# Two attention blocks on one core: the order in which an operation's several semaphore waits are stated

## The chip, the cores and the metric

The kernel runs on one core of a Trainium2 chip. The metric is the time of one execution on the device in microseconds (us); the number given for a kernel is the median of several runs. The engines are named as in the profile: PE is TensorE, PEld its weight loads, DVE is VectorE, ACT is ScalarE, POOL is GpSimd, SP is SyncE, which here only issues transfers.

## The reference

Two independent blocks are computed, and their outputs are put side by side along the last axis.

```python
def _A_ref(x, wqkv, wo):                      # x: 1 x 2048 x 1024, 32 heads of 32
    qkv = (x @ wqkv).reshape(B, S, 3, H, Dh).transpose(2, 0, 3, 1, 4)
    q, k, v = qkv[0], qkv[1], qkv[2]
    p = softmax(einsum('bhqd,bhkd->bhqk', q, k) * Dh ** -0.5)
    o = einsum('bhqk,bhkd->bhqd', p, v)
    return o.transpose(0, 2, 1, 3).reshape(B, S, D) @ wo

def _B_ref(x, wq, wk, wv, wo, beta):          # 4 segments of 512 rows, causal inside each
    for s in range(4):
        p = softmax(einsum('bhqd,bhkd->bhqk', qs, ks) * scale + mask)
        a_dot = einsum('bhqk,bhkd->bhqd', p, vs)
        num, den = phi(qs) @ M, phi(qs) @ z + 1e-6      # memory of the segments before
        o = g * num / den + (1 - g) * a_dot             # g = sigmoid(beta), per head
        M, z = M + phi(ks)^T @ vs, z + sum(phi(ks))
    return o @ wo                                       # phi(t) = t + 1 if t > 0 else exp(t)
```

## The kernel before

Everything is computed in pieces of a few tenths of a microsecond to one microsecond. Attention runs in sets of four tiles of 128 keys by 512 columns: PE writes the scores into PSUM (L1190; eight matmuls of 256 columns, their operands in KQ_A or KQ_B), ACT takes the exponential of 1024 columns at a time into P (L1288), and PE multiplies P with V (L1401) and with ones (L1408) for the sums. For block A one tile in some sets goes another way: DVE copies the scaled scores into Y (L1236), POOL squares them into Z (L1245) and turns Z into Pc (L1246), which stands for the exponential. Between the sets PE does the projections, each as runs of matmuls of 512 columns (L829 and, with other shapes, L1764 and L1866) that DVE copies out of PSUM (L1608, L1876), and the output products. Six PSUM banks in three slots serve the scores, two banks the projections and sums; a bank is written again when its reader has read it, so that PE waits for ACT or DVE, and these for PE. Weights (W_A, W_B, Wv_B, Wo_B) come by DMA on SP's queue, into one or two buffers.

What each engine does, and in which order, is settled when the program is built. `Prog.op` records every operation with the operations it depends on; `schedule` sets the order on each engine from planned durations, `rearrange` shifts it by a table, and `retime` gives each operation its planned start and end. `programs` then makes each engine's list of waits and operations. An operation needs what its dependencies on other engines (and, where needed, its own) have done. The dependencies are sorted by the time at which the plan has them met; going through them from the last to the first, a semaphore is noted in `need` only if nothing noted or waited for before already tells that it is met. So `need` begins with the wait that is planned to be met last. Its entries become `("w", semaphore, value)` items ahead of the operation, and `emit` turns each into a `wait_ge` in that order (`run_split` for ACT, whose list can branch).

About 390 operations of PE, 156 of DVE and 120 of POOL have more than one wait; ACT has 9 on the way that is run (it has a second list of the same work for data that the first does not suit), SP none.

## Time and profile before

| | us |
|---|---|
| median of 3 runs | 1057.81 |
| lowest, highest | 1056.15, 1058.79 |
| span of the profiled execution | 1056.3 |
| PE busy | 1023.3 (97%) |
| ACT busy | 1001.5 (95%) |
| POOL busy | 724.7 (69%) |
| DVE busy | 703.4 (67%) |

The span goes from the first to the last instruction of the profiled execution; the time of that execution is not listed apart from the runs. The granted TensorE clock is full over the whole span. The ends of matmuls are modelled, so that a busy PE is not one at its peak. Instructions that only wait are not among the profile's rows: what they cost shows in the distance between the end of what was waited for and the start of what waited. Times in the timeline are from the start of the span, and a row gives start, duration, engine, line, operation, output and input, count, and in brackets the idle time before it with what ended it ("issue" where the profile finds no releaser).

### The profile page before, as it was taken

Reading aid. Unit: us, or ns where it says so; the run is one execution under the profiler, and the core shown is the slowest. Engines: PE = TensorE matmul, PEld = TensorE weight load, DVE = VectorE, ACT = ScalarE, POOL = GpSimd, SP = SyncE. Lnnn points to the kernel's source line nnn. Section 1 sums busy time; section 2 is a strip of 40 time slices with the busy share of each in tenths; the row PEclk is TensorE's granted clock in tenths of the full one; section 3 lists DMA queues with packets and bytes.
Section 4 is the critical chain, followed back from the end, with each engine's and each line's share of the span. In section 5 each row is a group of like instructions: output and inputs, shape, how many; then the busy total and the mean of one; then the engine's idle time right before and its main releaser. Section 6 shows DMA issues by size and latency. Waiting matters only on the chain.

```text
span 1056.3 us, 54941 instructions
## 1 busy us (share of the span) xinstructions
PE 1023.3 (97%) x25091; PEld 551.2 (52%) x25092; DVE 703.4 (67%) x1451; ACT 1001.5 (95%) x1193; POOL 724.7 (69%) x999
## 2 busy tenths in 40 slices
PE   9999999999999999999999999999999999999998
PEld 4456455566555454556555445556555445445544
DVE  3457577666656878696755879777646887674444
ACT  5999999999999999898999999999999999999995
POOL 1005567666766888888956899888755878985551
PEclk9999999999999999999999999999999999999999
DMA  9213351007112530033241221133041433122002
GB/s 175 47 43 93 68 138 28 16 13 160 49 41 70 123 85 17 3 62 92 67 113 44 78 65 38 27 75 91 27 113 35 125 102 113 33 68 73 28 29 66
DMA packets 172377, 72.24 MB, mean 68 GB/s; under 512 B 135536, under 2 KB 170352, under 8 KB 172144
## 3 DMA queue, kind: packets, MB, share of 16 engines
q1 hardware_dynamic: 169776, 67.93, 26.3%
q8 instruction: 197, 3.23, 1.3%
q10 hardware_dynamic: 2368, 0.79, 0.3%
q14 instruction: 36, 0.29, 0.1%
HBM read 45.36 MB, written 11.80 MB: 54 GB/s over the span
## 4 chain that ended last, share of the span: by engine, by line
PE 56%; ACT 32%; DVE 4%; POOL 3%; SPq 3%; issue 1%; DMA 0%; ACTq 0%; POOLq 0%; DVEq 0%
ACT P L1288 32%; PE ps L829 27%; PE ps L1190 11%; PE ps L1401 8%; PE ps L1408 8%; SPq L1572 2%; POOL Z L1245 2%; DVE Y L1236 1%; PE ps L1866 1%; PE ps L1638 1%; POOL Pc L1246 1%; DVE T L1515 1%; DMA W_A<-in_A_wqkv_dram 0%; DVE PKQ_B L1925 0%; POOL P L1317 0%
## 5 line engine op out<-in xcount | busy, mean ns | idle before, releaser
L1288 ACT ACTIVATE P<-ps 128x1024 bf16<-128x1024 f32 (+1 forms) x1178 | 991.5, 999 | 33.6 <-PE ps L1190 18.7
L1245 POOL TENSOR_TENSOR Z<-Y 128x512 f32<-128x512 f32 x287 | 304.2, 1062 | 202.2 <-DVE Y L1236 177.7
L1408 PE MATMUL ps<-P,onesb 128*32 128x256 bf16 (+1 forms) x4386 | 300.8, 270 | 0.7 <-issue 0.6
L1401 PE MATMUL ps<-P,V_A 128*32 128x256 bf16 x3618 | 257.7, 274 | 0.7 <-issue 0.3
L1236 DVE TENSOR_SCALAR Y<-ps 128x512 f32<-128x512 f32 x239 | 163.7, 685 | 110.1 <-PE ps L1190 90.5
L1190 PE MATMUL ps<-KQ_A 32*128 32x256 bf16 x4096 | 204.1, 272 | 12.4 <-ACT P L1288 5.5
L1246 POOL TENSOR_SCALAR Pc<-Z 128x512 bf16<-128x512 f32 x239 | 155.6, 654 | 11.0 <-PE ps L1190 0.2
L1190 PEld LDWEIGHTS ps<-KQ_A 32*128 32x128 bf16 x4096 | 62.8, 92 | 163.9 <-ACT P L1288 108.7
L1408 PEld LDWEIGHTS ps<-P,onesb 128*32 128x32 bf16 x4386 | 128.8, 96 | 30.1 <-issue 14.8
L829 PE MATMUL ps<-xT_B,W_B 128*32 128x512 bf16 (+1 forms) x2132 | 138.7, 372 | 0.8 <-DVE OT_B L1948 0.2
L829 PE MATMUL ps<-xT_A,W_A 128*32 128x512 bf16 (+1 forms) x2020 | 131.4, 370 | 2.2 <-DMA W_A<-in_A_wqkv_dram 1.1
L1401 PEld LDWEIGHTS ps<-P,V_A 128*32 128x32 bf16 x3618 | 108.1, 96 | 34.3 <-issue 14.3
L1401 PE MATMUL ps<-Pc,V_A 128*32 128x256 bf16 x478 | 123.1, 273 | 0.4 <-ACT P L1288 0.2
L1408 PE MATMUL ps<-Pc,onesb 128*32 128x256 bf16 x478 | 122.8, 273 | 0.0
L1317 POOL TENSOR_SCALAR_AFFINE_SELECT P<-P 128x768 bf16<-128x768 bf16 (+1 forms) x96 | 76.3, 803 | 34.7 <-ACT P L1288 33.1
L1515 DVE STREAM_TRANSPOSE T<-ps 128x512 f32<-128x512 f32 x122 | 86.3, 708 | 14.0 <-PE ps L1408 11.9
L829 PEld LDWEIGHTS ps<-xT_B,W_B 128*32 128x32 bf16 x2132 | 50.3, 96 | 45.5 <-issue 19.6
L829 PE MATMUL ps<-Wo_B,OT_B 128*32 128x512 bf16 (+1 forms) x1080 | 71.6, 370 | 0.2 <-DVE rc L1518 0.2
L829 PE MATMUL ps<-Wv_B,xT_B 128*32 128x512 bf16 (+1 forms) x1096 | 70.3, 367 | 0.2
L829 PEld LDWEIGHTS ps<-xT_A,W_A 128*32 128x32 bf16 x2020 | 47.4, 96 | 42.1 <-issue 12.5
L1533 POOL TENSOR_TENSOR T<-T,rc 128x256 bf16<-128x256 f32 x74 | 48.9, 663 | 29.6 <-DVE rc L1518 25.8
L1608 DVE CAST KQ_A<-ps 128x512 bf16<-128x512 f32 x60 | 41.3, 689 | 40.5 <-PE ps L829 40.1
(109 smaller groups left out, 1201.0 us busy)
## 6 DMA issues: line engine op xcount, KB each, us to landing
Wv_B<-in_B_wv_dram SPq DMA_DIRECT2D x32, 256.0 KB, 3.5
W_B<-in_B_wk_dram SPq DMA_DIRECT2D x32, 256.0 KB, 3.3
W_B<-in_B_wq_dram SPq DMA_DIRECT2D x32, 256.0 KB, 4.1
Wo_B<-in_B_wo_dram SPq DMA_DIRECT2D x32, 256.0 KB, 3.5
out_dram<-outsb SPq DMA_DIRECT2D x56, 128.0 KB, 1.9
W_A<-in_A_wqkv_dram SPq DMA_DIRECT2D x14, 256.0 KB, 3.6
ot_a_scratch<-OTst SPq DMA_DIRECT2D x52, 64.0 KB, 2.3
xT_A<-ot_a_scratch SPq DMA_DIRECT2D x6, 512.0 KB, 4.8
```

Of the source, the lines that this page charges most:

```text
L829: ins = e.matmul(out[r], w[:, r], x, start=start, stop=stop, tile_position=(0, 32 * t), skip_group_check=True)
L1190: ins = e.matmul(out, kap, qap, start=st, stop=True, tile_position=(32 * h, 0), skip_group_check=True)
L1236: o = self.dve(lambda e: e.tensor_scalar(Y[:, :], src, SCALE, MID, ALU.mult, ALU.add), 512, key - 9.0, [self.bank[bank]], [rY], fixed=0.15)
L1245: self.pool(lambda e: e.tensor_tensor(Z[:, :], Y[:, :], Y[:, :], ALU.mult), 512, key, [rY], [rZ], rate=0.58)
L1246: return self.pool(lambda e: e.tensor_scalar(dst, Z[:, :], C2, REST, ALU.mult, ALU.add), 512, key, [rZ], [rP], rate=TS_RATE)
L1288: a = self.act(guarded if early and not free else lambda e: e.activation(dst, src, ACT.Exp, scale=SCALE), cols, key, rd, wr, fixed=EXP_FIXED)
L1317: self.pool(lambda e: e.affine_select(v, v, pattern=pat, compare_op=ALU.is_ge, fill=0.0, base=0, channel_multiplier=-1), 2 * nd * P, key + ...
L1401: ins = e.matmul(self.ps[32 * h:32 * h + 32, 512 * obk + q0:512 * obk + q0 + nq], v, p, start=first, stop=last, tile_position=(0, 32 * h), ...
L1408: ins = e.matmul(self.ps[32 * h:32 * h + 32, lcol + q0:lcol + q0 + nq], self.onesb[:, 0:32], p, start=False, stop=last, tile_position=(0, ...
L1515: self.dve(lambda e: e.transpose(T2[:, :], src), 512, k - NORM_K, [obk.res], [ro, rl], fixed=0.17)
L1533: self.pool(lambda e: e.tensor_tensor(half.rearrange("p (b r) -> p b r", r=32), ov, bc, ALU.mult), QC, k, [ro, rr], [rl], rate=0.435)
L1608: self.dve(lambda e: e.tensor_copy(dst, src), 512, key, [self.at(b)], rdst, fixed=0.155)
```

## The change

The waits noted in `need` are stated in the order in which they were noted, the one planned to be met last first. Before, they were stated from the other end. Which semaphores and values are waited for, the operations, their order and their buffers stay as they were.

```diff
                     for x in reversed(deps):
                         s, v = target(x)
                         if k.get(id(s), 0) < v:
                             need.append((s, v))
...
-                    for s, v in reversed(need):
+                    for s, v in need:
                         prog[e].append(("w", s, v))
```

On PE, about 98 us into the span, a set of scores (L1190) and a projection of block B (L829) stand close together, both with two waits. s_ACT, s_DVE and s_POOL are the semaphores that count what these engines have done; d_WB01 is that of the DMA which brings the second piece of W_B. Before:

```order
L1190 MATMUL ps<-KQ_A 128x256 [waits s_ACT,s_DVE]
L1190 MATMUL ps<-KQ_A 128x256 x7
L1401 MATMUL ps<-Pc,V_A 32x256
L1401 MATMUL ps<-P,V_A 32x256 x3
L1408 MATMUL ps<-Pc,onesb 32x256
L1408 MATMUL ps<-P,onesb 32x256 x3
L829 MATMUL ps<-xT_B,W_B 32x512 [waits s_DVE,d_WB01]
L829 MATMUL ps<-xT_B,W_B 32x512 x3
L1401 MATMUL ps<-P,V_A 32x256 x4
```

And after:

```order
L1190 MATMUL ps<-KQ_A 128x256 [waits s_DVE,s_ACT]
L1190 MATMUL ps<-KQ_A 128x256 x7
L1401 MATMUL ps<-Pc,V_A 32x256
L1401 MATMUL ps<-P,V_A 32x256 x3
L1408 MATMUL ps<-Pc,onesb 32x256
L1408 MATMUL ps<-P,onesb 32x256 x3
L829 MATMUL ps<-xT_B,W_B 32x512 [waits d_WB01,s_DVE]
L829 MATMUL ps<-xT_B,W_B 32x512 x3
L1401 MATMUL ps<-P,V_A 32x256 x4
```

For the scores, ACT's semaphore stood ahead and DVE's on the first matmul's weight load; now DVE's stands ahead and ACT's is the load's own. For the projection, DVE's stood ahead and the DMA's was the load's own; now the DMA's stands ahead.

On POOL, about 876 to 882 us into the span, squares (Z) and their second step (Pc) stand in turn. A square waits for DVE, which makes Y, and for POOL itself, which must have read the Z that is written again. Before:

```order
L1245 TENSOR_TENSOR Z<-Y 128x512 [waits s_DVE,s_POOL]
L1246 TENSOR_SCALAR Pc<-Z 128x512 [waits s_POOL]
L1245 TENSOR_TENSOR Z<-Y 128x512 [waits s_POOL,s_DVE]
L1246 TENSOR_SCALAR Pc<-Z 128x512
L1245 TENSOR_TENSOR Z<-Y 128x512 [waits s_DVE,s_POOL]
L1246 TENSOR_SCALAR Pc<-Z 128x512 [waits s_POOL]
L1520 TENSOR_SCALAR rc<-rc,gc 128x8
L1245 TENSOR_TENSOR Z<-Y 128x512 [waits s_POOL,s_DVE]
```

And after:

```order
L1245 TENSOR_TENSOR Z<-Y 128x512 [waits s_POOL,s_DVE]
L1246 TENSOR_SCALAR Pc<-Z 128x512 [waits s_POOL]
L1245 TENSOR_TENSOR Z<-Y 128x512 [waits s_DVE,s_POOL]
L1246 TENSOR_SCALAR Pc<-Z 128x512
L1245 TENSOR_TENSOR Z<-Y 128x512 [waits s_POOL,s_DVE]
L1246 TENSOR_SCALAR Pc<-Z 128x512 [waits s_POOL]
L1520 TENSOR_SCALAR rc<-rc,gc 128x8
L1245 TENSOR_TENSOR Z<-Y 128x512 [waits s_DVE,s_POOL]
```

In each pair the two names have changed places; which of the two was ahead before differs from square to square, as the plan has one or the other met last. Operations with a single wait are as they were.

## The prediction

> **What bounds the kernel now.** I read the page first, then the list of waits, the chain of waits in order of time, and last the timeline in windows of a fifth of a microsecond, where two neighbouring rows show how long an engine takes to start once it is released.

> ```profile
> span 1056.3 us, 54941 instructions
> PE 1023.3 (97%) x25091; PEld 551.2 (52%) x25092; DVE 703.4 (67%) x1451; ACT 1001.5 (95%) x1193; POOL 724.7 (69%) x999
> PE 56%; ACT 32%; DVE 4%; POOL 3%; SPq 3%; issue 1%; DMA 0%; ACTq 0%; POOLq 0%; DVEq 0%
> ```

> Two engines are nearly full, ACT with exponentials and PE with everything that feeds and follows them, and the chain that ended last changes between the two, with short pieces of DVE and POOL between. No engine alone is the bound. Such a program pays for every hand-over on that chain: an operation ends, its semaphore rises, and the next engine starts a little later.

> ```profile
> ACT P L1288 <- PE ps L1190: 18.7, 37, 1.2
> ACT P L1288 <- PE ps L1408: 11.6, 18, 1.6
> PEld ps L1190 <- ACT P L1288: 130.9, 368, 1.1
> PEld ps L829 <- issue: 62.2, 289, 0.5
> ```

> ACT stood for PE only 55 times (37 + 18), for 30.3 us together; PE's weight loads stood for ACT 368 times, and those of L829 289 times for 62.2 us where the profile names no releaser ("issue"). What the change touches is the last tenth of a microsecond of such waits.

> ```profile
> 45.42 8.36 ACT P L1288 x9
> ...
> 920.69 113.88 ACT P L1288 x139
> ```

> These are the first and the last of 17 pieces of over 4 us in which the chain runs through exponentials back to back, 336 us together. There no hand-over counts; it counts in the 720 us that are left.

> **What the change moves.** It moves no operation, adds none and takes none away. An operation with several waits keeps the same ones, in the opposite order. The rows on the change above show how the built program holds them: one wait sits on the operation itself, the others stand ahead of it as wait instructions. Before, the semaphore planned to be met last stands ahead, alone, and the early one sits on the operation; after the change it is the other way round. So the question is what it costs when the late semaphore is met by the instruction of its own, and not by the operation.

> PE first. A weight load with one wait, after the DVE operation that releases it:

> ```profile
> 40.78 0.69 DVE L1608 CAST KQ_A<-ps 128x512 bf16<-128x512 f32 x1 [2.02 <-PE ps L829]
> 41.53 0.12 PEld L829 LDWEIGHTS ps<-xT_A,W_A 128*32 128x32 bf16 x8 [0.20 <-DVE KQ_A L1608]
> 1047.56 0.69 DVE L2109 TENSOR_TENSOR KQ_B<-ps,KQ_B 128x512 bf16<-128x512 f32 x1 [0.53 <-PE ps L829]
> 1048.30 0.10 PEld L829 LDWEIGHTS ps<-W_A,xT_A 128*32 128x32 bf16 x4 [0.21 <-DVE KQ_B L2109]
> ```

> DVE ends at 41.47 and 1048.25; the load starts 0.06 and 0.05 later. Now loads with two waits, where DVE's semaphore is the late one and stands ahead:

> ```profile
> 77.72 0.69 DVE L1608 CAST KQ_A<-ps 128x512 bf16<-128x512 f32 x1 [0.67 <-PE ps L829]
> 78.53 0.13 PEld L1866 LDWEIGHTS ps<-Wv_A,xT_A 128*128 128x128 bf16 x2 [0.27 <-issue]
> 97.67 0.69 DVE L1608 CAST KQ_B<-ps 128x512 bf16<-128x512 f32 x1
> 98.47 0.13 PEld L829 LDWEIGHTS ps<-xT_B,W_B 128*32 128x32 bf16 x4 [0.15 <-issue]
> 983.57 0.68 DVE L1236 TENSOR_SCALAR Y<-ps 128x512 f32<-128x512 f32 x1
> 984.36 0.15 PEld L1190 LDWEIGHTS ps<-KQ_A 32*128 32x128 bf16 x8 [0.38 <-ACT P L1288]
> ```

> DVE ends at 78.41, 98.36 and 984.25, the loads start 0.12, 0.11 and 0.11 later: **0.06 us more** for each. The load at 98.47 is the one shown with its waits in the section on the change.

> DVE shows the difference inside one kind of operation, Y at L1236, each with a wait for PE and one for POOL:

> ```profile
> 877.65 1.04 POOL L1245 TENSOR_TENSOR Z<-Y 128x512 f32<-128x512 f32 x1
> 878.73 0.69 DVE L1236 TENSOR_SCALAR Y<-ps 128x512 f32<-128x512 f32 x1 [0.95 <-POOL Z L1245]
> 918.26 1.04 POOL L1245 TENSOR_TENSOR Z<-Y 128x512 f32<-128x512 f32 x1
> 919.41 0.69 DVE L1236 TENSOR_SCALAR Y<-ps 128x512 f32<-128x512 f32 x1 [2.46 <-POOL Z L1245]
> ```

> POOL ends at 878.69 and 919.30, and Y starts 0.04 and 0.11 later. In the first the plan had PE's semaphore last, so POOL's sits on the operation; in the second POOL's stands ahead. The difference is **0.07 us**. POOL the same, Z with one wait and then with two:

> ```profile
> 911.87 0.69 DVE L1236 TENSOR_SCALAR Y<-ps 128x512 f32<-128x512 f32 x1 [0.44 <-PE ps L1190]
> 912.64 1.04 POOL L1245 TENSOR_TENSOR Z<-Y 128x512 f32<-128x512 f32 x1 [0.19 <-DVE Y L1236]
> 117.24 0.68 DVE L1236 TENSOR_SCALAR Y<-ps 128x512 f32<-128x512 f32 x1
> 118.07 1.04 POOL L1245 TENSOR_TENSOR Z<-Y 128x512 f32<-128x512 f32 x1 [2.02 <-DVE Y L1236]
> 878.73 0.69 DVE L1236 TENSOR_SCALAR Y<-ps 128x512 f32<-128x512 f32 x1 [0.95 <-POOL Z L1245]
> 879.57 1.08 POOL L1245 TENSOR_TENSOR Z<-Y 128x512 f32<-128x512 f32 x1 [0.29 <-DVE Y L1236]
> ```

> Y ends at 912.56, 117.92 and 879.42; Z starts 0.08, 0.15 and 0.15 later, again **0.07 us**.

> [...]

> **The sum.** I followed the chain back from ACT's last instruction through the trace, at each step to what came last: a release with the delays above, or the instruction before on the same engine. On it lie 145 starts with several waits that were released by the wait standing ahead: 97 on PE (first 78.53; 984.36 is the last that DVE releases), 28 on DVE (919.41 among them), 20 on POOL (first 118.07, last 879.57). At the full price that is 97 x 0.06 + 28 x 0.07 + 20 x 0.07 = 5.8 + 2.0 + 1.4 = 9.2 us. Two things come off. Of the 145, 35 (26 on PE, 9 on DVE) lie inside the 17 long pieces above, where the profile's own chain has ACT running through; I count those at nothing, the exponential before being what is late next. That leaves 71 x 0.06 + 19 x 0.07 + 20 x 0.07 = 4.3 + 1.3 + 1.4 = 7.0 us. And on 11 places of the chain (6 on PE, 3 on DVE, 2 on POOL; 878.73 is one) the early-planned semaphore came last in fact: there the change puts the late one ahead, which costs 6 x 0.06 + 5 x 0.07 = 0.7 us. **7.0 - 0.7 = 6.3 us saved.**

> Costed at nothing: ACT, whose few operations with several waits are not on the chain; SP, whose waits keep their order; and the wait that now stands ahead, which by plan was met earlier, so that it is passed while the engine still works at what is before it. Where that cover is missing, the price is the 0.06 to 0.07 us just counted. Nothing new is queued behind a waiting instruction: the same engine waits for the same pair, and behind it stands what stood there.

> The span, 1056.3, is 1.5 us under the median of the runs shown, 1057.81, and the fastest run took 1056.15, so the profiled execution was an ordinary one and the saving may be taken off the median: 1057.8 - 6.3 = **1051.5 us**. Differences under 0.3%, 3.2 us, cannot be told from none here.

> **The rivals.**

> *The gain is taken up by the other chains (0.12).* PE and ACT are both nearly full, so beside the chain run others that are almost as long. For it speaks that ACT stands for PE only 55 times. If the end moves only where ACT stood, and every second of these has one dear start ahead of it, the gain is 55 x 0.06 / 2 = 1.6 us: 1056.2, which would read as no change. Against it speaks that the 110 places are spread over the whole span and that each shortens PE's chain and ACT's alike.

> *The plan's order is wrong more often than now (0.10).* When some engines start earlier, semaphores that lay 0.1 us apart may change places, and an operation whose early-planned one now comes last gains nothing. If a third of the 110 flip, 110 / 3 x 0.063 = 2.3 us are lost: 4.0 saved, 1053.8.

> *The late semaphore standing ahead is the cheap way, and the change makes it dear (0.05).* As the source reads, the wait stated last is next to the operation, and the change moves the late one away from it. If the last stated wait sat on the operation in what the chip executes, the 145 places would each become dearer by 0.06 to 0.07: 9.2 us, less the 0.7 of the 11 places that would then gain, 1066.3. It decides if the dear starts above have another reason than the place of the wait, such as a longer decode of this kind of load; L1236, where the same operation starts after 0.04 and after 0.11, speaks against that. [...]

> *It does nothing (0.03).* If the waits are sorted again on the way to the chip, both programs are one: 1057.8.

> **How the numbers follow.** My forecast has 0.70, and 1051.5 is its value. The range reaches from the full price of all 145 places, 1057.8 - 9.2 = 1048.6, to the absorbed gain, 1056.2; that leaves out the last two rivals, 0.08, and the tails. Faster by over 0.3% (under 1054.6): the forecast and the flipped order, 0.80. Within 0.3%: absorbed or nothing, 0.15. Slower: 0.05.

> **What would show it.** In the changed profile the load of the second W_B piece (98.47 before) should start 0.05 after its CAST, Y at L1236 behind POOL 0.04 and Z behind Y 0.08 in nearly every case with two waits; the gain should grow evenly up to about 900 us, and little in the last 130. ACT's 30.3 us of standing for PE should fall by some microseconds, and the 62.2 us of L829's loads put down to "issue" too. The working is wrong if these starts are as short as I say and the span still stays within 3 us (then the hand-overs were not on what sets the end), and the reading of the order is wrong if the starts at 0.11 have grown in number.

## The result, and the profile after

The changed kernel took 1051.33 us (median of 6 runs, 1050.78 to 1052.71), the kernel before, beside it, 1058.17 us (6 runs, 1056.15 to 1060.88). The ratio is 0.9937, its 95% interval 0.9924 to 0.9949: by this ratio 6.7 us faster, 5.4 to 8.0. The same kernel, run again as the last of the experiments, gave 0.9934 (0.9920 to 0.9947).

The page of the changed kernel first, its span, the engines, and the chain by engine:

```profile
span 1049.4 us, 54941 instructions
PE 1019.2 (97%) x25091; PEld 548.0 (52%) x25092; DVE 703.0 (67%) x1451; ACT 999.0 (95%) x1193; POOL 725.7 (69%) x999
PE 62%; ACT 29%; DVE 3%; SPq 2%; POOL 1%; issue 1%; DMA 1%; ACTq 0%; DVEq 0%; POOLq 0%
```

The same work, as full as before, in a span that is 6.9 us shorter. DVE and POOL have a smaller part of the chain than before (4% together, from 7%), ACT too (29%, from 32%), and PE a larger one (62%, from 56%). The list of waits, with us in total, times, and the longest:

```profile
PEld ps L1190 <- ACT P L1288: 118.7, 343, 1.2
PEld ps L829 <- issue: 50.3, 235, 1.5
...
ACT P L1288 <- PE ps L1190: 16.1, 31, 1.2
...
ACT P L1288 <- PE ps L1408: 10.0, 17, 1.6
```

ACT stands for PE 26.1 us in place of 30.3 (28.6 in a second profile of the changed kernel). The weight loads of L829 for which the profile named no releaser are 54 fewer and stand 11.9 us less. I read these as loads whose late semaphore was met by a wait instruction ahead of them, which is not among the profile's rows; the first two loads shown next, of L1866 and L829, are of this kind.

Now the starts themselves, at the places of the prediction. PE's loads with two waits, in the timeline of the changed kernel:

```profile
77.84 0.69 DVE L1608 CAST KQ_A<-ps 128x512 bf16<-128x512 f32 x1 [0.76 <-PE ps L829]
78.59 0.11 PEld L1866 LDWEIGHTS ps<-Wv_A,xT_A 128*128 128x128 bf16 x2 [0.21 <-DVE KQ_A L1608]
...
97.52 0.69 DVE L1608 CAST KQ_B<-ps 128x512 bf16<-128x512 f32 x1
98.26 0.10 PEld L829 LDWEIGHTS ps<-xT_B,W_B 128*32 128x32 bf16 x4
...
976.56 0.68 DVE L1236 TENSOR_SCALAR Y<-ps 128x512 f32<-128x512 f32 x1
977.39 0.15 PEld L1190 LDWEIGHTS ps<-KQ_A 32*128 32x128 bf16 x8 [0.35 <-DVE Y L1236]
```

DVE ends at 78.53 and 98.21, and the loads start 0.06 and 0.05 later, where it was 0.12 and 0.11; for the first the profile now names DVE as the releaser where it had said "issue". The third, 977.39, starts 0.15 after DVE's end at 977.24, where it was 0.11. After the loads of L829 ahead of it (at 976.94, and at 983.88 before) it starts 0.45 later, where it was 0.48: so the work ahead seems to hold it now, and of the 0.06 only 0.03 is gained here. Of the three loads that the prediction shows, two have the full price. DVE's Y behind POOL, and POOL's Z behind Y:

```profile
911.57 1.04 POOL L1245 TENSOR_TENSOR Z<-Y 128x512 f32<-128x512 f32 x1
912.65 0.69 DVE L1236 TENSOR_SCALAR Y<-ps 128x512 f32<-128x512 f32 x1 [2.38 <-POOL Z L1245]
...
871.25 1.09 POOL L1245 TENSOR_TENSOR Z<-Y 128x512 f32<-128x512 f32 x1
872.44 0.69 DVE L1236 TENSOR_SCALAR Y<-ps 128x512 f32<-128x512 f32 x1 [1.00 <-POOL Z L1245]
873.21 1.14 POOL L1245 TENSOR_TENSOR Z<-Y 128x512 f32<-128x512 f32 x1 [0.29 <-DVE Y L1236]
```

Y at 912.65 (919.41 before) starts 0.04 after POOL, not 0.11. Y at 872.44 (878.73 before) is the one whose early-planned semaphore comes last: it starts 0.10 after POOL, where it was 0.04. The two have changed places, to a hundredth. Z starts 0.08 after Y's end at 873.13, where it was 0.15. The same holds over the whole trace, counted from the rise of the semaphore. Of POOL's starts on a release by DVE, 46 of 152 came 0.12 to 0.14 us after it, and now 2 of 149. Of DVE's starts on a release by POOL, 7 of 34 came 95 or 96 ns after it, and now 1 of 36, the Y at 872.44; nearly all others came after 23 to 25 ns.

Last, where in the span the time went. Pieces of the chain that are the same stretch of work in both kernels, first before, then after:

```profile
221.26 16.68 ACT P L1288 x19
...
449.40 23.33 ACT P L1288 x27
...
666.68 23.24 ACT P L1288 x27
...
808.00 24.56 ACT P L1288 x29
...
1045.35 6.29 PE ps L829 x116
```

```profile
219.85 16.68 ACT P L1288 x19
...
447.14 23.16 ACT P L1288 x27
...
661.99 23.16 ACT P L1288 x27
...
802.43 24.57 ACT P L1288 x29
...
913.84 27.80 ACT P L1288 x33
...
1038.52 6.29 PE ps L829 x116
```

The stretches begin 1.4, 2.3, 4.7, 5.6 and 6.8 us earlier. The run of exponentials that began at 920.69 begins at 913.84, 6.85 earlier, and 125 us later the lead is still 6.83. The gain is made in small steps all along, and none in the last eighth.

### The profile page after: what moved, and what is told of

The parts are those of the page before. It is cut to its first block, busy times and chain, and to the rows that moved or that the text cites. A ratio compares the mean times of both kernels' runs of the same rounds, so it can differ in the third digit from the quotient of the medians.

```text
span 1049.4 us, 54941 instructions
## 1 busy us (share of the span) xinstructions
PE 1019.2 (97%) x25091; PEld 548.0 (52%) x25092; DVE 703.0 (67%) x1451; ACT 999.0 (95%) x1193; POOL 725.7 (69%) x999
## 4 chain that ended last, share of the span: by engine, by line
PE 62%; ACT 29%; DVE 3%; SPq 2%; POOL 1%; issue 1%; DMA 1%; ACTq 0%; DVEq 0%; POOLq 0%
PE ps L829 30%; ACT P L1288 29%; PE ps L1190 12%; PE ps L1401 9%; PE ps L1408 9%; SPq L1572 2%; PE ps L1866 1%; DVE Y L1236 1%; PE ps L1638 1%; DVE T L1515 1%; DMA W_A<-in_A_wqkv_dram 1%; POOL Z L1245 0%; POOL P L1317 0%; DVE KQ_B L1608 0%; DVE sqB L1621 0%
## 5 line engine op out<-in xcount | busy, mean ns | idle before, releaser
L1288 ACT ACTIVATE P<-ps 128x1024 bf16<-128x1024 f32 (+1 forms) x1178 | 989.0, 1020 | 29.4 <-PE ps L1190 16.1
L1245 POOL TENSOR_TENSOR Z<-Y 128x512 f32<-128x512 f32 x287 | 305.4, 1067 | 195.3 <-DVE Y L1236 182.3
L1408 PE MATMUL ps<-P,onesb 128*32 128x256 bf16 (+1 forms) x4386 | 300.1, 270 | 0.0
L1236 DVE TENSOR_SCALAR Y<-ps 128x512 f32<-128x512 f32 x239 | 163.8, 685 | 108.7 <-PE ps L1190 90.0
L1190 PE MATMUL ps<-KQ_A 32*128 32x256 bf16 x4096 | 204.1, 273 | 12.1 <-ACT P L1288 6.6
L1190 PEld LDWEIGHTS ps<-KQ_A 32*128 32x128 bf16 x4096 | 62.1, 92 | 164.6 <-ACT P L1288 95.0
L1408 PEld LDWEIGHTS ps<-P,onesb 128*32 128x32 bf16 x4386 | 128.7, 96 | 30.0 <-issue 14.5
L829 PE MATMUL ps<-xT_B,W_B 128*32 128x512 bf16 (+1 forms) x2132 | 138.8, 372 | 0.1
L829 PE MATMUL ps<-xT_A,W_A 128*32 128x512 bf16 (+1 forms) x2020 | 131.3, 370 | 1.8 <-DMA W_A<-in_A_wqkv_dram 1.3
L1408 PE MATMUL ps<-Pc,onesb 128*32 128x256 bf16 x478 | 122.8, 273 | 0.0
L1515 DVE STREAM_TRANSPOSE T<-ps 128x512 f32<-128x512 f32 x122 | 86.3, 707 | 13.0 <-PE ps L1408 11.6
L829 PE MATMUL ps<-Wo_B,OT_B 128*32 128x512 bf16 (+1 forms) x1080 | 71.6, 370 | 0.0
L829 PEld LDWEIGHTS ps<-xT_B,W_B 128*32 128x32 bf16 x2132 | 48.4, 96 | 44.0 <-issue 12.0
L829 PE MATMUL ps<-Wv_B,xT_B 128*32 128x512 bf16 (+1 forms) x1096 | 70.3, 367 | 0.0
L829 PEld LDWEIGHTS ps<-xT_A,W_A 128*32 128x32 bf16 x2020 | 47.0, 96 | 41.7 <-issue 12.2
L1608 DVE CAST KQ_A<-ps 128x512 bf16<-128x512 f32 x60 | 41.4, 689 | 40.5 <-PE ps L829 40.2
```

Of the source, the lines that this page charges most:

```text
L829: ins = e.matmul(out[r], w[:, r], x, start=start, stop=stop, tile_position=(0, 32 * t), skip_group_check=True)
L1190: ins = e.matmul(out, kap, qap, start=st, stop=True, tile_position=(32 * h, 0), skip_group_check=True)
L1236: o = self.dve(lambda e: e.tensor_scalar(Y[:, :], src, SCALE, MID, ALU.mult, ALU.add), 512, key - 9.0, [self.bank[bank]], [rY], fixed=0.15)
L1245: self.pool(lambda e: e.tensor_tensor(Z[:, :], Y[:, :], Y[:, :], ALU.mult), 512, key, [rY], [rZ], rate=0.58)
L1288: a = self.act(guarded if early and not free else lambda e: e.activation(dst, src, ACT.Exp, scale=SCALE), cols, key, rd, wr, fixed=EXP_FIXED)
L1408: ins = e.matmul(self.ps[32 * h:32 * h + 32, lcol + q0:lcol + q0 + nq], self.onesb[:, 0:32], p, start=False, stop=last, tile_position=(0, ...
```

## The experiments

My theory: a semaphore that is met last costs 0.06 to 0.07 us more when a wait instruction ahead of the operation meets it than when the operation's own wait does, and this counts where the start lies on what sets the end. The rivals were that the price has to do with the number of waits and not with their place, that other chains take the gain up, and that one engine brings all of it. Gains below are against the kernel before, 1058.1 to 1058.2 us, each with its interval. The cuts of code are edits of the kernel before.

**One engine at a time.** Each of three kernels turns the waits round on one engine only:

```diff
-                    for s, v in reversed(need):
+                    for s, v in need if e == "PE" else reversed(need):
```

and the same with "DVE" and with "POOL".

> The waits are turned round on PE alone. My theory (each late semaphore met by a wait standing ahead costs 0.06 to 0.07 us, and it counts where the start lies on the chain): 71 x 0.06 less 6 x 0.06 = 3.9 us faster, ratio 0.9963; with the full price of all 97 places 5.5 us, 0.9948. Rival (only the 55 stretches in which ACT stands for PE count, 1.6 us in all): ratio 0.9985. Rival (the gain of the whole change comes from DVE and POOL, whose waits feed PE): ratio 1.000.

Measured: 1053.87 us, ratio 0.9962 (0.9949 to 0.9975), 4.0 us faster (2.6 to 5.4). This is the theory's 3.9. The full price of all 97 places, 5.5, lies just outside the interval; the 1.6 us of the rival that counts only ACT's stretches lies well outside, and so does the rival that gives PE nothing.

> The waits are turned round on DVE alone. My theory: 19 x 0.07 less 3 x 0.07 = 1.1 us faster, ratio 0.999; at the full price of 28 places 1.8 us, 0.9983. Rival (DVE, 67% busy, has slack that takes it up): 1.000. A gain of over 3 us would mean that DVE's starts hold up far more than the chain shows.

Measured: 1055.81 us, ratio 0.9979 (0.9970 to 0.9987), 2.2 us faster (1.4 to 3.2). Twice what I had counted for DVE: the 1.1 lies outside the interval, and so does none. The full price of 28 places, 1.8, is inside.

> The waits are turned round on POOL alone. My theory: 20 x 0.07 less 2 x 0.07 = 1.3 us faster, ratio 0.9988. Rival (POOL has slack that takes it up): 1.000.

Measured: 1057.20 us, ratio 0.9991 (0.9980 to 1.0002), 1.0 us faster (0.2 slower to 2.1 faster). It agrees with 1.3 and cannot be told from none. The three together are 7.2 us, the whole change 6.7: within what the runs can tell, the engines' parts add up.

**The chain alone, and everything else.** A table holds the numbers of the 110 operations that the prediction counted; in one kernel only these are turned round, in the other all but these (`reversed(need) if o.num in TURN else need`).

```diff
-                    for s, v in reversed(need):
+                    for s, v in need if o.num in TURN else reversed(need):
```

> Of the some 680 operations with several waits only the 110 are turned round that the chain of the trace before names outside its long runs of exponentials (71 on PE, 19 on DVE, 20 on POOL). My theory, if the chain sets the end: 7.0 us faster, ratio 0.9934, as much as the whole change or a little more. Rival (many chains are almost as long, and to shorten one leaves the next): at most half, 3.5 us, 0.9967 or more.

Measured: 1053.38 us, ratio 0.9961 (0.9946 to 0.9975), 4.1 us faster (2.6 to 5.7). The theory's 7.0 lies outside the interval, and the rival's 3.5 inside. A sixth of the operations brings some 60% of the gain, so that the chain is where most of it lies. That the rest is taken up by other chains that are late next is the rival's reading, which fits but is not shown by this run alone.

> The other half of the run on the chain's 110 places: all operations with several waits are turned round except those 110. My theory as it now stands (the end depends on a bundle of chains of almost equal length, so that the 110 alone gave 4.1 us and the rest of the change's 6.3 us lies outside them): 2.2 us faster than the kernel before, ratio 0.998. Rival (the two parts only work together, since a bundle ends later unless all of it is shortened): 1.000. Rival (the prediction's step: outside the 110 there are only the dearer places): 0.7 us slower, 1.0007.

Measured: 1057.68 us, ratio 0.9992 (0.9983 to 1.0001), 0.8 us faster (0.1 slower to 1.8). The theory's 2.2 lies outside, and so does the prediction's 0.7 slower; the rival that gives nothing lies just inside. The two parts are 4.9 us together, the whole 6.7. That fits a bundle of chains of nearly the same length, which ends earlier only if all of it is shortened; as the intervals of the parts still reach the whole, it is not shown.

**The long pieces alone.** The same edit with the 177 operations that start inside the 17 long runs of exponentials.

> Only the 177 operations with several waits are turned round that start inside the 17 long pieces of the trace before in which the chain runs through exponentials back to back (104 on PE, 52 on DVE, 19 on POOL, 2 on ACT). My theory, as the prediction counted it: nothing, ratio 1.000. Rival, which the run on the chain's 110 places has made likelier (there 4.1 us came of 7.0, so that 2.2 us of the whole change's 6.3 lie elsewhere): the 35 starts of my own chain in these pieces count like the others, 26 x 0.06 + 9 x 0.07 = 2.2 us faster, ratio 0.998.

Measured: 1057.46 us, ratio 0.9990 (0.9982 to 0.9999), 1.1 us faster (0.1 to 1.9). Half of what the rival gives: its 2.2 lies outside the interval, and so does the prediction's nothing, though only just.

**The place of a wait against the number of waits.** Two kernels, both the changed one with a second wait on each operation of PE that has one (leaving out the first 41 operations); the semaphore value waited for in addition is reached at the very start. In the first it stands ahead and the real wait stays on the operation; in the second they are the other way round. Both have 1017 instructions more.

```diff
-                    need = []
+                    need, idle = [], [(sems["POOL"], 1)]
...
-                    for s, v in reversed(need):
+                    for s, v in need + idle if e == "PE" and len(need) == 1 and at[e] > 40 else need:
```

and in the second `idle + need`.

> The changed kernel, and on PE each operation with one wait gets a second one, for a semaphore value that POOL reaches at the very start; it stands ahead, and the real wait stays on the operation. My theory (a wait that is met long before costs nothing, because PE's sequencer passes it while the array is busy): as the changed kernel, ratio 0.994 to the kernel before. Rival (each wait instruction costs PE's sequencer its 0.06 us wherever it stands): about 1000 more of them, at least the 111 single-wait starts of the chain x 0.06 = 6.7 us, ratio 1.000 or more.

Measured: 1056.53 us, ratio 0.9986 (0.9977 to 0.9996), 5.2 us behind the changed kernel as it was timed first, and 4.9 behind the kernel of the order by measurement below, which was timed beside this one. Neither theory: not free, and not 0.06 us on each start either. The reason that the theory gives, that PE's sequencer passes such a wait while the array is busy, is not shown by this. The load that the prediction showed with one wait, in the timeline of this kernel:

```profile
41.62 0.69 DVE L1608 CAST KQ_A<-ps 128x512 bf16<-128x512 f32 x1 [2.02 <-PE ps L829]
...
42.37 0.12 PEld L829 LDWEIGHTS ps<-xT_A,W_A 128*32 128x32 bf16 x8 [0.20 <-DVE KQ_A L1608]
```

It starts 0.06 after DVE's end at 42.31, as with one wait. So the 5 us are not on this start. PE's own waits without a releaser in this profile are

```profile
PE ps L829 <- issue: 1.8, 4, 0.8
PE ps L1190 <- issue: 1.4, 3, 1.0
PE ps L1408 <- issue: 0.8, 2, 0.6
PE ps L1401 <- issue: 0.6, 1, 0.6
PE ps L1764 <- issue: 0.2, 1, 0.2
```

4.8 us in eleven places, against 0.7 us in two in the profile of the changed kernel above; but a second profile of the changed kernel had 4.1 us in five places, at a span of 1051.7. So such stalls come and go from run to run. Put beside the changed kernel's trace exponential by exponential, this one's last exponentials come 7.2 us later, and 5.7 of that come in four jumps: 2.2 us between 243 and 262 us, 1.2 at about 608, 1.0 at about 730 and 1.3 at about 865, with smaller steps elsewhere. At the first three stand stalls of the list, at 247 to 257, at 607 and at 728 to 734. The second profile of the changed kernel falls behind in the same way, by 3.0 us about two stalls of 1.4 us at 871 and 877. So in these traces most of the time goes at a few places and not a little on every start; what causes the stalls, and whether the added instructions bring more of them, stays open.

> The same two waits as in the run with the idle wait ahead, but the real wait stands ahead and the one that is met from the start sits on the operation. My theory (the price is on the late semaphore standing ahead): the 111 starts of PE on the chain that have one wait each become 0.06 us later, 6.7 us, and since more starts come onto the chain as it grows, up to all of PE's 459 that start on a release, 27.5 us; ratio to the kernel before 1.000 to 1.020, and 6.7 to 27.5 us behind the run with the idle wait ahead. Rival (the place of the wait does not matter, only the number): the same time as that run.

Measured: 1078.35 us, ratio 1.0181 (1.0165 to 1.0196), 21.8 us behind the run before by the medians. Same waits, same number of instructions, only their places changed, and the time moves by three times what the whole change is worth. The theory's 6.7 to 27.5 us behind that run hold it, and the rival's same time does not. The same load in this kernel's timeline:

```profile
40.69 0.69 DVE L1608 CAST KQ_A<-ps 128x512 bf16<-128x512 f32 x1 [2.10 <-PE ps L829]
...
41.50 0.14 PEld L829 LDWEIGHTS ps<-xT_A,W_A 128*32 128x32 bf16 x6 [0.26 <-issue]
```

It starts 0.12 after DVE's end at 41.38, and "issue" is back as the releaser. This settles the theory against the rival of the mere number.

**The same on DVE.** The idle wait ahead, on DVE's operations with one wait (`e == "DVE"` in the edit above).

> The changed kernel, and each operation of DVE with one wait gets a second one that is met from the start and stands ahead (937 more wait instructions on DVE). On PE 1017 such waits cost about 5 us in a few stalls without a releaser. Theory (that price is that of PE's own stream of 50,000 instructions, whose sequencer has no time to spare; DVE's has 1451 and much time): as the changed kernel, ratio 0.994. Rival (any wait instruction costs about 0.005 us on its engine): 937 x 0.005 = 4.6 us behind the changed kernel, 0.998.

Measured: 1051.87 us, ratio 0.9946 (0.9932 to 0.9960), 1.3 us behind the changed kernel timed beside it, within what the runs can tell. 4.6 us would have shown. 937 waits more on DVE that are met early cost nothing that can be measured. The reason that the theory gives, the time that PE's and DVE's sequencers have to spare, is not shown by this.

**The order by measurement.** The changed kernel, with 95 operations turned back (`reversed(need) if o.num in TURN else need`) by a table of those whose early-planned semaphore came last in the trace.

> The changed kernel, but the 95 operations for which the trace of the changed kernel shows that the early-planned semaphore came last are turned back (78 on PE, 13 on DVE, 2 on POOL, 2 on ACT). My theory: the 11 places on the chain that became dearer are cheap again, 0.7 us faster than the changed kernel, 7.0 us against the kernel before, ratio 0.993. Rival (other chains take it up): as the changed kernel, 0.9937.

Measured: 1051.68 us, ratio 0.9943 (0.9930 to 0.9955). As the changed kernel; a gain of 0.7 us would be too small to see in these runs.

**Fewer wait instructions.** On PE the early one of two waits goes to the nearest of up to eight operations ahead that has none and that the plan starts 0.5 us or more after the semaphore is met. Of `hoist` only the condition and the insertion are shown.

```diff
-                            need.append((s, v))
+                            need.append((s, v)); when.append(x.end + x.lat)
...
-                    for s, v in reversed(need):
+                    for s, v in hoist(prog[e], need, when, e):
...
+                if p[j - 1][0] == "o" and t + 0.5 <= p[j][1].start:
+                    p.insert(j, ("w", *w))
```

> The changed kernel, but on PE the early of two waits is put on one of the up to eight operations before, the nearest that has no wait and that the plan starts at least 0.5 us after the semaphore is met, so that 162 of PE's 398 wait instructions go. Theory (wait instructions on PE cost 5 us per 1017 of them): 162 x 0.005 = 0.8 us faster than the changed kernel, ratio 0.993 to the kernel before. Rival (a wait that is met early costs nothing, and the plan is off by more than 0.5 us in places, so that the operation ahead now stands): as the changed kernel or some us behind it, 0.994 to 0.998.

Measured: 1053.39 us, ratio 0.9957 (0.9943 to 0.9971), by the ratios 2.4 us behind the changed kernel timed beside it; the two intervals just overlap. No gain, perhaps a loss. The theory's 0.8 us is not borne out, but the run does not test the price per wait instruction by itself, as an operation ahead may now stand for a wait that was moved to it.

> The changed kernel again, on the same chip and against the same runs of the kernel before as the other three: ratio 0.994, for comparison.

Measured: 1050.89 us, ratio 0.9934 (0.9920 to 0.9947). No version that was run beats the changed kernel.

## Why the prediction was right, point by point

**The price of the place** was right: 0.06 us on PE, 0.07 on DVE and POOL, read from neighbouring rows before and gone after, and back again, in the other direction, in the one Y shown where the plan's order is wrong. On PE the run with the late wait ahead shows the same price by itself, 0.12 against 0.06 at the same load.

**Which wait sits where** was right, and it decided the sign. The source alone, read as it stands, gives the rival that would have been 8.5 us slower.

**The sum**, 6.3 us against 6.7 measured, was right in total and uneven in its terms. PE's 3.9 measured 4.0, POOL's 1.3 measured 1.0, DVE's 1.1 measured 2.2. One step that failed is "35 (26 on PE, 9 on DVE) lie inside the 17 long pieces above, where the profile's own chain has ACT running through; I count those at nothing": turned round alone, the operations in these pieces gave 1.1 us, 0.1 to 1.9. The trace before shows why nothing was too little. An exponential that stood for PE starts 23 or 24 ns after PE's semaphore rises, in 52 of 58 such waits. Inside the long pieces 54 of 407 exponentials also start 23 or 24 ns after a rise (the delays next to these, 21, 22 and 25 ns, have one case or none each), although the row ahead of them reaches past their start. So the profile counts no idle time there and puts the step down to ACT, and the pieces are not all ACT's own.

**The chain as the thing that sets the end** held only in part, and this term was off by more. The 110 places alone gave 4.1 us of the 7.0 that the sum has for them, 2.9 too few. The long pieces gave 1.1 more than counted, so that the two errors go against each other but do not cancel. The parts on the chain and off it are 4.9 us together; the other 1.8 us of the whole change either lie in the noise of the parts or come only when all places are turned round, which is not shown. That the total came within half a microsecond was in part luck.

**The dearer places**, 0.7 us, stay open: they are there in the rows (872.44), but turning them back gave nothing that the runs can tell.

**Costed at nothing**: ACT, SP and the early wait ahead. The early wait ahead leaves no trace in the starts of the loads shown, 0.06 us after DVE in the run with the idle wait ahead and 0.05 at 98.26 in the changed kernel, as with one wait; that it is passed while the engine still works at what is before it was an estimate, as waits have no rows. And 1017 more of them on PE cost 5.2 us in all. Both kernels have the same number, so it did not touch the prediction.

**The course** was as forecast: a gain in small steps up to about 900 us, roughly even, and nothing in the last 130. ACT's standing for PE is down by 4.2 us, in the second profile by 1.7.

## What to carry to other kernels

Where an operation waits for several semaphores, see in the built program which wait the operation carries and which stand ahead of it, and give the operation the one that is met last: here that was worth 0.6% for a change of one word. Read the price from two neighbouring rows, the end of the releaser and the start of the released, with one wait and with two. A count along one chain gave the size of the gain here in part by luck, and it was not the list of what brings it: the places on the chain alone gave 4.1 us, all places 6.7. And a piece of the chain that runs through one engine's rows without idle time may still wait for another engine: compare the starts with the rises of the semaphore before counting it at nothing.

## What the runs showed of the hardware that was not expected

Wait instructions on PE that are met long before are not free in the mass: 1017 more of them cost 5.2 us (ratio 0.9986 against 0.9937), while 937 more on DVE cost nothing that could be measured (0.9946 against 0.9934, timed side by side). The load looked at starts as short after its release as before, 0.06 us, and in the one trace with the added waits most of the time, 5.7 of 7.2 us, goes in four jumps, three of them at stalls of PE of up to 1.0 us without a releaser. The cause of these stalls is open.

No idle time ahead of an exponential is no proof that ACT did not wait: in the trace before, 54 of the 407 in the long pieces start 23 or 24 ns after PE's semaphore, as released ones do, while the row of the exponential ahead still runs.
